# Score broadcasts on GpSimd's queue, row copies for the last batch only, and scatters issued later, in a windowed attention with a mixture-of-depths stage

## The chip, the cores and the metric

The kernel runs on one core of a Trainium2 chip. The metric is the device time of one execution in microseconds, the median over several runs. The profile is one execution recorded by the hardware profiler; its span (148.8 us for the kernel before) is a little shorter than the device time of the same run (150.53 us).

The engines are named as in the profile: PE is TensorE (matrix products; PEld its weight loads), DVE is VectorE, ACT is ScalarE, POOL is GpSimd, SP is SyncE, which here only issues transfers. Each engine takes its instructions in program order, so an instruction that waits holds up everything behind it on that engine.

## What is computed

Attention with a few sink keys and a sliding window, over 4 batches, 8 heads, 768 positions and head size 64; then a feed-forward layer on the 128 rows of each batch that score highest against a gate vector.

```python
keep = (pos[None, :] < 4) | ((rel >= 0) & (rel < 128))       # 4 sinks, a window of 128
a = softmax(where(keep, q @ k.T / 8, -1e9));  x = a @ v       # (B, S, 512) once heads are joined
scores = einsum('bsd,d->bs', x, w_gate)
out = x.copy()
for b in range(4):
    top = indices of the 128 largest scores[b]
    ye = maximum(x[b, top] @ w1, 0) @ w2                      # 512 -> 1024 -> 512
    out[b, top] = x[b, top] + sigmoid(scores[b, top])[:, None] * ye
```

## The kernel before

**Steps.** Attention is cut into 30 steps of 128 query rows: steps 0 to 11 for batch 0 (in two halves of the heads), then six steps for each of the batches 1, 2 and 3 (12 to 17, 18 to 23, 24 to 29). In step i TensorE first forms the scores of step i + 2 (`step_scores`), ScalarE takes their exponentials, then TensorE forms the sums over the values of step i (`values`, line 262, with the sink part at line 272) in PSUM banks 4 and 5. VectorE normalizes them (`norm`, lines 295 and 298) into a tile x, and the next step's `values` can't overwrite the banks before that. VectorE then forms the gate scores of the 128 rows (`gate_score`, line 302). SyncE stores x to the output (`store`, line 503).

**An order written by hand.** Everything else is hung on the steps: `before(i, ...)` runs ahead of step i, `middle(i, ...)` between its scores and its values, `at(i, ...)` after its normalization, `late(i, ...)` at its end. Loads of K and Q (line 129) and V (148, 152) go out on SyncE, K and Q are cast on GpSimd (line 141), transposed on TensorE (line 172), and the key columns of the sinks copied by GpSimd (`sink_keys`, line 186). The compiled program gives SyncE's transfers eight completion semaphores in turn: each transfer waits for the one eight places ahead of it.

**Ranking.** To find the 128 best rows of a batch, each score is compared with all 768 of the batch. For batches 0 and 1 the scores go to memory and come back on all 128 partitions: `bounce_out` (line 306) writes the column tile scol to a row srow in DRAM, `bounce_in` (line 309) reads it back into sbc, the same row on every partition. Then `rank_c` (line 312, VectorE) counts for 128 rows at a time how many scores are larger. The bounces of batch 0 are placed at steps 12 and 13, its ranks from step 15 on; those of batch 1 at steps 18 and 19, its ranks from step 20 on. For batches 2 and 3 the row is made on the chip step by step: `spread` (line 316, TensorE into bank 2, then a copy by ScalarE) and `compare` (lines 323 and 325).

**Choosing.** `select` (line 345) turns ranks into one-hot matrices, and `chosen` (line 351) multiplies them with a small table tok of token numbers and scores into a PSUM bank; VectorE copies the result to ch (line 354) and forms the row indices. `gather` (line 376) fetches the 128 chosen rows with an indirect transfer of GpSimd. For batch 0 it reads the output itself; for batches 1 to 3 it reads a second copy of the rows, xrow, which `store` writes beside the output (line 505), with indices local to the batch (idl). For these batches VectorE forms two sets of indices: idl for the gather and idx for the later scatter.

**Feed-forward.** `ffn_cast` (line 381, GpSimd), `ffn_in` (386), `ffn_1` (394), `ffn_2` (401) and `ffn_out` (406) follow two to five steps later; ffn_out adds the rows (y) and at once scatters them into the output (line 408, an indirect transfer of GpSimd). Batch 0 does this in steps 24 to 26, batch 1 in 27 to 29, batch 2 from step 29 on, batch 3 after the last step. The weights are cast while loading, on GpSimd's queue (lines 521 and 525).

Of the kernel before, what the change touches and what calls it, by code (L numbers as in the profile page):

```python
# [8 lines left out]
FP32 = mybir.dt.float32  # L9
BF16 = mybir.dt.bfloat16  # L10
I32 = mybir.dt.int32
U32 = mybir.dt.uint32
# [3 lines left out]
B = 4  # L16
H = 8
S = 768
D = 64
HP = H // 2  # L20
NB = S // 128
DM = H * D
# [11 lines left out]
def kernel(  # L34
# [14 lines left out]
    pe, dve, act, pool, sp = nc.tensor, nc.vector, nc.scalar, nc.gpsimd, nc.sync  # L49
# [35 lines left out]
    tok = [one([128, NB, 4], BF16, f"tok{i}") for i in range(B)]  # L85
    gt = [one([128, 1], FP32, f"gt{i}") for i in range(B)]
    idx = [one([128, 1], U32, f"idx{i}") for i in range(B)]
    xe = [one([128, DM], FP32, f"xe{i}") for i in range(3)]
# [17 lines left out]
    tk_i = one([128, B + 1, NB], I32, "tk_i")  # L106
    flat = out.rearrange("b s d -> (b s) d")
    srow = tc.dram_tile([B, S], FP32, name="srow")
    xrow = [None] + [tc.dram_tile([S, DM], FP32, name=f"xrow{i}") for i in range(1, B)]
    idl = [None] + [x0[:, NB - 2, 8 * i:8 * i + 1].bitcast(U32) for i in range(1, B)]  # L110

    class State:
        def __init__(self, b):
# [7 lines left out]
    st = [State(b) for b in range(B)]  # L121
# [181 lines left out]
                                 op0=ALU.mult, op1=ALU.add, accum_out=st[b].scol[:, j:j + 1])  # L303

    def bounce_out(b):
        sp.dma_start(out=srow[b, :].rearrange("(p c) -> p c", c=NB), in_=st[b].scol[:, :])

    def bounce_in(b):
        sp.dma_start(out=sbc[:, :], in_=srow[b, :].partition_broadcast(128))

    def rank_c(b, c):
        dve.tensor_scalar(out=junk[:, :].bitcast(BF16)[:, 0:S], in0=sbc[:, :], scalar1=st[b].scol[:, c:c + 1],  # L312
# [35 lines left out]
    def chosen(b, bank, e=E):  # L348
        t = tok[b]
        for c in range(NB):  # L350
            pe.matmul(out=ps[:, bank, 0:4], lhsT=e[:, c, :], rhs=t[:, c, :],
                      start=(c == 0), stop=(c == NB - 1))
        ch = jp.tile([128, 4], FP32, name="ch", tag="ch")
        dve.tensor_copy(out=ch[:, :], in_=ps[:, bank, 0:4])
        dve.tensor_scalar(out=(idl[b] if b else idx[0])[:, :], in0=ch[:, 0:1], scalar1=128.0, scalar2=ch[:, 1:2],
                          op0=ALU.mult, op1=ALU.add)
        if b:
            chl = x0[:, NB - 2, 32:33]
            dve.tensor_scalar_add(out=chl[:, :], in0=ch[:, 1:2], scalar1=float(b * S))
            dve.tensor_scalar(out=idx[b][:, :], in0=ch[:, 0:1], scalar1=128.0, scalar2=chl[:, 0:1],  # L360
                              op0=ALU.mult, op1=ALU.add)
        return ch

    def gate(b, ch):
        g = gt[b]
        dve.tensor_tensor(out=g[:, :], in0=ch[:, 2:3], in1=ch[:, 3:4], op=ALU.add)
        act.activation(out=g[:, :], in_=g[:, :], func=ACT.Exp, scale=-1.0)

    def gate_end(b):
        g = gt[b]  # L370
        dve.tensor_scalar_add(out=g[:, :], in0=g[:, :], scalar1=1.0)
        dve.reciprocal(out=g[:, :], in_=g[:, :])

    def gather(b):
        src, ix = (xrow[b], idl[b]) if b else (flat, idx[0])
        pool.indirect_dma_start(out=xe[b % 3][:, :], out_offset=None, in_=src[0:S, :],
                                in_offset=bass.IndirectOffsetOnAxis(ap=ix[:, 0:1], axis=0),
                                bounds_check=S - 1, oob_is_err=False)

    def ffn_cast(b):  # L380
        pool.tensor_copy(out=xeb[:, :], in_=xe[b % 3][:, :])

    def ffn_in(b, bank):
        trp = ps[:, bank, :].bitcast(BF16).rearrange("p (c n) -> p c n", c=8)
        for dc in range(4):
            pe.transpose(out=trp[:, dc, :], in_=xeb[:, dc * 128:(dc + 1) * 128], identity=ident_b[:, :])
        act.copy(out=xeT[:, :, :], in_=trp[:, 0:4, :])  # L387
# [10 lines left out]
    def ffn_2(b, half, bank):  # L398
        for f in range(4):
            fc = 4 * half + f  # L400
            pe.matmul(out=ps[:, bank, :], lhsT=hT[:, fc, :], rhs=w2_sb[:, fc, :],
                      start=(fc == 0), stop=(fc == 7))

    def ffn_out(b, bank):
        y = jp.tile([128, DM], FP32, name="y", tag="y")
        dve.scalar_tensor_tensor(out=y[:, :], in0=ps[:, bank, :], scalar=gt[b][:, 0:1], in1=xe[b % 3][:, :],  # L406
                                 op0=ALU.mult, op1=ALU.add)
        pool.indirect_dma_start(out=flat[0:(b + 1) * S, :],
                                out_offset=bass.IndirectOffsetOnAxis(ap=idx[b][:, 0:1], axis=0),
                                in_=y[:, :], in_offset=None, bounds_check=(b + 1) * S - 1, oob_is_err=False)  # L410

    with tc.manual_schedule():
        dve.memset(zb[:, :], 0.0)
# [11 lines left out]
                           base=0, pattern=[[-1, 128]], channel_multiplier=1)  # L425
# [47 lines left out]
        def at(i, f):  # L473
            todo.setdefault(i, []).append(f)
# [7 lines left out]
        def before(i, f):  # L482
            early.setdefault(i, []).append(f)
# [13 lines left out]
        xt = {}  # L497

        def store(i):
            b, j, g = steps[i]  # L500
            if g == 0:
                return
            sp.dma_start(out=out[b, j * 128:(j + 1) * 128, :], in_=xt[(b, j)])
            if b:
                sp.dma_start(out=xrow[b][j * 128:(j + 1) * 128, :], in_=xt[(b, j)])


        arrived = {}
# [19 lines left out]
        def choose(b, bank, e=E):  # L528
            keep[b] = chosen(b, bank, e)
            gate(b, keep[b])  # L530
            gather(b)
# [23 lines left out]
        at(26, lambda: choose(1, 3))  # L555
        late(26, lambda: select(E2, rankl[0], 0, NB))
        at(27, lambda: gate_end(1))
        at(27, lambda: choose(2, 2, E2))
        at(28, lambda: gate_end(2))
        for b in range(B - 1):  # L560
            at((12, 18, 24)[b], lambda b=b: token_cols(b))
# [22 lines left out]
        def ffn(b, i):  # L584
            before(i, lambda: ffn_cast(b))
            at(i, lambda: ffn_in(b, Y))
            at(i + 1, lambda: ffn_1(b, 0, Y + 1))
            at(i + 1, lambda: ffn_1(b, 1, Y))
            for half in range(2):
                at(i + 2, lambda half=half: ffn_2(b, half, Y + 1))  # L590
            at(i + 2, lambda: ffn_out(b, Y + 1))
        ffn(0, 24)
        ffn(1, 27)
        before(29, lambda: ffn_cast(2))
        at(29, lambda: ffn_in(2, Y))

# [4 lines left out]
                           pattern=[[-NSINK, HP]], channel_multiplier=1)  # L601
        pool.affine_select(out=o, in_=o, compare_op=ALU.is_ge, fill=0.0, base=NSINK - 1,
                           pattern=[[NSINK, HP]], channel_multiplier=-1)
# [4 lines left out]
                        in_=own4[0:16, :].unsqueeze(1).to_broadcast((16, 2 * B, HP)))  # L608
        pool.tensor_copy(out=vsk[64:80, :, :, :, :].rearrange("p b e h d -> p (b e h d)"),
                         in_=vsk[0:16, :, :, :, :].rearrange("p b e h d -> p (b e h d)"))  # L610

        for i, (b, j, g) in enumerate(steps):
            for f in early.get(i, []):
                f()
            if i:
                store(i - 1)
            step_scores(i + 2)
            for f in mid.get(i, []):
                f()
            heads = range(4) if g is None else (2 * g, 2 * g + 1)  # L620
            values(b, j, heads, X, g or 0)
            if b == 0:
                x = x0[:, j, :]
            else:
                x = xp.tile([128, DM], FP32, name="x", tag="x")[:, :]
            norm(x, heads, X)
            if i == len(steps) - 1:
                gate_score(b, j, x)
            for f in todo.get(i, []):
                f()  # L630
            if g != 0:
                xt[(b, j)] = x
                if i < len(steps) - 1:
                    gate_score(b, j, x)
                if b == B - 1:
                    pool.tensor_copy(out=xb[:, j, :], in_=x)  # L636
            for f in todo_late.get(i, []):
                f()
            if i == 5:
                pool.iota(iota_i[:, :], pattern=[[1, 128]], base=0, channel_multiplier=0)  # L640
                pool.iota(tk_i[:, 0:B, :], pattern=[[0, B], [1, NB]], base=0, channel_multiplier=0)
                pool.iota(tk_i[:, B, :], pattern=[[0, NB]], base=0, channel_multiplier=1)
            if i == 8:
                dve.tensor_copy(out=iota_f[:, :], in_=iota_i[:, :])
                for n in range(B):
                    dve.tensor_copy(out=tok[n][:, :, 0], in_=tk_i[:, n, :])
                    dve.tensor_copy(out=tok[n][:, :, 1], in_=tk_i[:, B, :])
        store(len(steps) - 1)

        b = B - 1  # L650
# [18 lines left out]
        choose(b, 2)  # L669
        ffn_2(2, 1, 0)  # L670
        ffn_out(2, 0)
        gate_end(b)
        ffn_1(b, 0, Y)
        ffn_1(b, 1, Y + 1)
        ffn_2(b, 0, 1)
        ffn_2(b, 1, 1)
        ffn_out(b, 1)


# [33 lines left out]
```

The softmax here doesn't subtract the row's maximum and nothing guards it: scores larger than these inputs give would overflow.

## Time and profile before

| | before |
|---|---|
| device time, median of 3 | 153.0 us (152.77 to 153.94) |
| span of the profiled run | 148.8 us |
| mean granted TensorE clock | 0.966 |
| busy: PE / DVE / ACT / POOL | 120.2 / 91.5 / 78.5 / 58.8 us |
| moved by DMA | 35.57 MB, mean 239 GB/s |
| SyncE's queue (q1) | 30.16 MB, 66.8% of the 16 DMA engines |
| GpSimd's queue (q0) | 4.23 MB, 13.6% |

Busy time doesn't add up to a bound: what counts is where the busiest engine waits, and for whom. The page gives, for each group of instructions, the idle time ahead of it and what ended it; a list of waits sums the same by pairs, and timelines show single instructions in order. The page's slices show that the DMA engines are busy nine tenths and more in most of the first 100 us:

```profile
PEclk9999999999999999999999997589999999999995
DMA  3999969987999999999999799899995346332031
```

Each digit is one fortieth of the span. The upper row is the clock that TensorE was granted in tenths, the lower row the busy share of the DMA engines. The clock has one dip, about 90 to 100 us from the start.

### The profile page before, as it was taken

What the parts mean: (1) busy time and instruction counts of PE and PEld (TensorE: products, weight loads), DVE (VectorE), ACT (ScalarE), POOL (GpSimd) and SP (SyncE); (2) the same over time, 40 slices, a digit from 0 to 9 for tenths busy, and PEclk for the clock granted to TensorE, in tenths of its full rate; (3) what the DMA queues carried; (4) which work ended last, traced back from release to release, by engine and by line L of the source; (5) the groups of instructions that cost most, each with busy time, mean ns of one, the idle gap of its engine ahead of it and who ended that gap; (6) DMA issues with size and microseconds to landing.
All of it is one profiled execution on the core that took longest, in us unless ns stands there. A gap on an engine that the chain in (4) does not pass through costs nothing. (4 is left out here: it accounts for less than half of the span.)

```text
span 148.8 us, 6421 instructions
## 1 busy us (share of the span) xinstructions
PE 120.2 (81%) x2755; PEld 91.6 (62%) x2759; DVE 91.5 (62%) x287; ACT 78.5 (53%) x106; POOL 58.8 (40%) x99
## 2 busy tenths in 40 slices
PE   6687989998989987669799920998989969977940
PEld 2255676787778866538588810776777558856810
DVE  6851172569438464098988306778996696688520
ACT  3169467598887875365746780055827232323310
POOL 8819404865504573343170401810111264412421
PEclk9999999999999999999999997589999999999995
DMA  3999969987999999999999799899995346332031
GB/s 100 376 222 361 213 173 365 341 207 194 286 291 375 335 240 317 352 347 348 268 327 316 221 257 317 218 194 172 279 275 195 143 148 216 141 141 77 3 138 70
DMA packets 43227, 35.57 MB, mean 239 GB/s; under 512 B 27184, under 2 KB 36400, under 8 KB 43200
## 3 DMA queue, kind: packets, MB, share of 16 engines
q1 hardware_dynamic: 40288, 30.16, 66.8%
q0 software_dynamic: 2368, 4.23, 13.6%
q10 hardware_dynamic: 544, 0.79, 1.5%
q8 instruction: 21, 0.34, 0.9%
q14 instruction: 6, 0.05, 0.1%
HBM read 25.20 MB, written 12.06 MB: 250 GB/s over the span
## 5 line engine op out<-in xcount | busy, mean ns | idle before, releaser
L251 ACT ACTIVATE pt<-ps 128x1024 f32<-128x1024 f32 x48 | 47.0, 1032 | 6.7 <-PE ps L229 6.0
L262 PE MATMUL ps<-vbuf,pt 64*64 64x65 f32 (+1 forms) x1440 | 47.6, 230 | 3.6 <-issue 2.9
L262 PEld LDWEIGHTS ps<-vbuf,pt 64*64 64x64 f32 (+1 forms) x1440 | 40.7, 139 | 15.3 <-issue 11.8
L141 POOL CAST kq<-raw 128x768 bf16<-128x768 f32 x28 | 23.4, 847 | 20.4 <-DMA raw<-in_k_dram 14.9
L295 DVE RECIPROCAL rz<-ps 128x8 f32<-128x8 f32 (+1 forms) x30 | 5.9, 196 | 29.1 <-PE ps L262 29.0
L272 PE MATMUL ps<-vsk,psk 64*64 64x260 f32 (+1 forms) x180 | 16.5, 359 | 8.6 <-DVE x L298 8.6
L213 PE MATMUL ps<-QT,KT 64*64 64x192 bf16 (+2 forms) x384 | 17.2, 243 | 5.0 <-ACT QT L179 2.6
L298 DVE TENSOR_TENSOR x<-ps,rz 128x256 f32<-128x256 f32 (+1 forms) x60 | 19.5, 366 | 1.6 <-DMA xrow<-x 0.4
L312 DVE TENSOR_SCALAR_CACHE_REDUCE junk<-sbc,scol 128x768 bf16<-128x768 f32 x12 | 12.2, 1013 | 12.3 <-DMA sbc<-srow 11.9
L302 DVE CUSTOM_DVE_ANT_0 junk<-x,wgb 128x512 f32<-128x512 f32 x24 | 18.0, 750 | 0.4
L186 POOL COPY ksk<-KT 64x4 bf16<-64x4 bf16 x32 | 8.7, 273 | 23.8 <-DVE KT L177 12.5
L179 ACT COPY QT<-ps 128x768 bf16<-128x768 bf16 x16 | 12.8, 801 | 7.9 <-PE ps L172 7.9
L213 PEld LDWEIGHTS <-KT 64*64 64x64 bf16 x384 | 10.3, 105 | 9.9 <-issue 6.0
L229 PE MATMUL ps<-mask,ident_b 64*64 64x256 bf16 (+1 forms) x208 | 15.0, 259 | 0.0
L172 PE MATMUL ps<-ident_b,kq 128*128 128x128 bf16 x192 | 13.6, 220 | 1.6 <-ACT kq L139 1.5
L272 PEld LDWEIGHTS ps<-vsk,psk 64*64 64x64 f32 x180 | 7.7, 135 | 10.3 <-DVE x L298 8.9
L172 PEld LDWEIGHTS <-kq 128*128 128x128 bf16 x192 | 11.1, 98 | 3.7 <-ACT kq L139 1.7
L318 ACT COPY sbl<-ps 128x128 f32<-128x128 f32 x12 | 3.1, 261 | 19.3 <-PE ps L316 19.3
L177 DVE COPY KT<-ps 128x768 bf16<-128x768 bf16 x10 | 9.5, 950 | 1.4 <-PE ps L172 1.4
L636 POOL CAST x<-x 128x512 bf16<-128x512 f32 x6 | 4.2, 703 | 15.1 <-DVE x L298 9.0
L394 PE MATMUL ps<-xeT,w_sb 128*128 128x128 bf16 x128 | 8.0, 219 | 0.7 <-ACT xeT L387 0.7
L394 PEld LDWEIGHTS <-w_sb 128*128 128x128 bf16 x128 | 7.4, 98 | 1.1 <-DVE y L406 0.9
(91 smaller groups left out, 133.1 us busy)
## 6 DMA issues: line engine op xcount, KB each, us to landing
out_dram<-x SPq DMA_DIRECT2D x24, 256.0 KB, 4.7
raw<-in_k_dram SPq DMA_DIRECT2D x15, 384.0 KB, 5.5
raw<-in_q_dram SPq DMA_DIRECT2D x15, 384.0 KB, 5.9
xrow<-x SPq DMA_DIRECT2D x18, 256.0 KB, 4.9
vbuf<-in_v_dram SPq DMA_DIRECT2D x33, 128.0 KB, 5.2
w_sb<-in_moe_w_dram POOLq DMA_DIRECT2D x4, 512.0 KB, 12.5
vbuf<-in_v_dram SPq DMA_DIRECT2D x2, 384.0 KB, 6.8
sbc<-srow SPq DMA_DIRECT2D x2, 384.0 KB, 6.6
```

What stands on the lines that cost most here:

```text
L141: (eng or pool).tensor_copy(out=o, in_=i)
L172: pe.transpose(out=trp[:, c, :], in_=src[:, c, :, :].rearrange("p h d -> p (h d)"), identity=ident_b[:, :])
L179: act.copy(out=o, in_=i)
L213: pe.matmul(out=sc[64 * m:64 * m + 64, e, a, o:o + n], lhsT=s.KT[r, hp, k0:k0 + 64], rhs=s.QT[r, hp, k0:k0 + n], start=a == 0, stop=False, ...
L229: pe.matmul(out=o, lhsT=ident_b[r, r], rhs=w[r].unsqueeze(1).to_broadcast((64, a.stop - a.start, 2, 64)), start=False, stop=True, skip_gro ...
L251: act.activation(out=po[:, gi, :, :, :], in_=sc[:, :, :, :], func=ACT.Exp, scale=0.125)
L262: pe.matmul(out=ps[64 * c:64 * c + 64, bank + be, hh * SK:hh * SK + SK], lhsT=p[i][rows, h, 64 * slot:64 * slot + 64], rhs=s.v[be][rows, h ...
L272: pe.matmul(out=ps[64 * c:64 * c + 64, bank + be, a * SK:z * SK], lhsT=s.psk[which][r, c, 64 * (j - 1):64 * j], rhs=vsk[r, b, be, a:z, :], ...
L298: dve.tensor_tensor(out=xo[:, e, :, :], in0=xg[:, e, :, 0:D], in1=rz[:, e, 0:n, :].to_broadcast((128, n, D)), op=ALU.mult)
L302: dve.tensor_tensor_reduce(out=junk[:, :], in0=x, in1=wgb[:, :], scale=1.0, scalar=0.0, op0=ALU.mult, op1=ALU.add, accum_out=st[b].scol[:, ...
L312: dve.tensor_scalar(out=junk[:, :].bitcast(BF16)[:, 0:S], in0=sbc[:, :], scalar1=st[b].scol[:, c:c + 1], scalar2=0.0, op0=ALU.is_gt, op1=A ...
L394: pe.matmul(out=hps[:, f, :], lhsT=w1_sb[:, dc, fc * 128:(fc + 1) * 128], rhs=xeT[:, dc, :], start=(dc == 0), stop=(dc == 3), skip_group_c ...
```

## The change

Four things are changed.

1. The two bounces of the scores of batches 0 and 1 are issued on GpSimd's queue instead of SyncE's, so that they needn't stand in SyncE's list.
2. Only the last batch keeps a second copy of its rows. Batches 1 and 2 gather from the output, with global row numbers: the table tok now holds 6b + c instead of c for batches 0 to 2, so that one set of indices serves gather and scatter.
3. A scatter to the output ahead of a gather from it would put the two in order. So the scatters of batches 0 and 1 are taken out of ffn_out and issued two steps after it for batch 0 (step 28) and at the end of the same step for batch 1 (step 29), after the gather of batch 2.
4. The third batch's `chosen` writes bank 3 instead of bank 2, which `spread` uses.

```diff
-    xrow = [None] + [tc.dram_tile([S, DM], FP32, name=f"xrow{i}") for i in range(1, B)]
-    idl = [None] + [x0[:, NB - 2, 8 * i:8 * i + 1].bitcast(U32) for i in range(1, B)]
+    xrow = tc.dram_tile([S, DM], FP32, name="xrow")
+    idl = x0[:, NB - 2, 0:1].bitcast(U32)
     def bounce_out(b):
-        sp.dma_start(out=srow[b, :].rearrange("(p c) -> p c", c=NB), in_=st[b].scol[:, :])
+        pool.dma_start(out=srow[b, :].rearrange("(p c) -> p c", c=NB), in_=st[b].scol[:, :])
     def bounce_in(b):
-        sp.dma_start(out=sbc[:, :], in_=srow[b, :].partition_broadcast(128))
+        pool.dma_start(out=sbc[:, :], in_=srow[b, :].partition_broadcast(128))
...
+        last = b == B - 1
-        dve.tensor_scalar(out=(idl[b] if b else idx[0])[:, :], ...)
-        if b:
+        dve.tensor_scalar(out=(idl if last else idx[b])[:, :], ...)
+        if last:
...
     def gather(b):
-        src, ix = (xrow[b], idl[b]) if b else (flat, idx[0])
+        src, ix, n = (xrow, idl, S) if b == B - 1 else (flat, idx[b], (b + 1) * S)
...
     def ffn_out(b, bank):
         ...
+    def scatter(b):
         pool.indirect_dma_start(out=flat[0:(b + 1) * S, :], ...)
...
     def store(i):
-            if b:
-                sp.dma_start(out=xrow[b][j * 128:(j + 1) * 128, :], in_=xt[(b, j)])
+            if b == B - 1:
+                sp.dma_start(out=xrow[j * 128:(j + 1) * 128, :], in_=xt[(b, j)])
...
-        at(27, lambda: choose(2, 2, E2))
+        at(27, lambda: choose(2, 3, E2))
...
+        late(28, lambda: scatter(0))
+        late(29, lambda: scatter(1))
...
-                pool.iota(tk_i[:, 0:B, :], pattern=[[0, B], [1, NB]], base=0, channel_multiplier=0)
+                pool.iota(tk_i[:, 0:B, :], pattern=[[NB, B], [1, NB]], base=0, channel_multiplier=0)
```

After the last step the scatters of batches 2 and 3 directly follow their ffn_out, as before.

More of the change, by code (lines that the diff above doesn't have):

```diff
@@ L354, in chosen @@
         dve.tensor_copy(out=ch[:, :], in_=ps[:, bank, 0:4])
-        dve.tensor_scalar(out=(idl[b] if b else idx[0])[:, :], in0=ch[:, 0:1], scalar1=128.0, scalar2=ch[:, 1:2],
+        last = b == B - 1
+        dve.tensor_scalar(out=(idl if last else idx[b])[:, :], in0=ch[:, 0:1], scalar1=128.0, scalar2=ch[:, 1:2],
                           op0=ALU.mult, op1=ALU.add)
-        if b:
+        if last:
             chl = x0[:, NB - 2, 32:33]
@@ L374, in gather @@
     def gather(b):
-        src, ix = (xrow[b], idl[b]) if b else (flat, idx[0])
-        pool.indirect_dma_start(out=xe[b % 3][:, :], out_offset=None, in_=src[0:S, :],
+        src, ix, n = (xrow, idl, S) if b == B - 1 else (flat, idx[b], (b + 1) * S)
+        pool.indirect_dma_start(out=xe[b % 3][:, :], out_offset=None, in_=src[0:n, :],
                                 in_offset=bass.IndirectOffsetOnAxis(ap=ix[:, 0:1], axis=0),
-                                bounds_check=S - 1, oob_is_err=False)
+                                bounds_check=n - 1, oob_is_err=False)
     def ffn_cast(b):
@@ L402, in ffn_2 @@
                       start=(fc == 0), stop=(fc == 7))
+    ys = {}
     def ffn_out(b, bank):
-        y = jp.tile([128, DM], FP32, name="y", tag="y")
+        y = ys[b] = jp.tile([128, DM], FP32, name="y", tag="y")
         dve.scalar_tensor_tensor(out=y[:, :], in0=ps[:, bank, :], scalar=gt[b][:, 0:1], in1=xe[b % 3][:, :],
                                  op0=ALU.mult, op1=ALU.add)
+    def scatter(b):
         pool.indirect_dma_start(out=flat[0:(b + 1) * S, :],
                                 out_offset=bass.IndirectOffsetOnAxis(ap=idx[b][:, 0:1], axis=0),
-                                in_=y[:, :], in_offset=None, bounds_check=(b + 1) * S - 1, oob_is_err=False)
+                                in_=ys[b][:, :], in_offset=None, bounds_check=(b + 1) * S - 1, oob_is_err=False)
     with tc.manual_schedule():
@@ L645 @@
                 for n in range(B):
-                    dve.tensor_copy(out=tok[n][:, :, 0], in_=tk_i[:, n, :])
+                    dve.tensor_copy(out=tok[n][:, :, 0], in_=tk_i[:, n % (B - 1), :])
                     dve.tensor_copy(out=tok[n][:, :, 1], in_=tk_i[:, B, :])
@@ L671 @@
         ffn_out(2, 0)
+        scatter(2)
         gate_end(b)
@@ L677 @@
         ffn_out(b, 1)
+        scatter(b)
 _INS = ['q', 'k', 'v', 'n_sink', 'window', 'moe_w_gate', 'moe_w1', 'moe_w2', 'moe_capacity']
```

## The prediction

> **What bounds the kernel now.** I read the busy shares first. TensorE is busy 81% of the span, so it sets the pace, and time is won where it stands still. The list of waits then shows who makes it stand still.
>
> ```profile
> PE 120.2 (81%) x2755; PEld 91.6 (62%) x2759; DVE 91.5 (62%) x287; ACT 78.5 (53%) x106; POOL 58.8 (40%) x99
> DVE junk L312 <- DMA sbc<-srow: 11.9, 2, 7.6
> PE ps L272 <- DVE x L298: 8.6, 5, 5.5
> ```
>
> Two waits of VectorE for the score broadcast make 11.9 us, the longer one 7.6. TensorE's waits for x (line 298, the normalization, also on VectorE) make 8.6, the longest 5.5. The timelines tie them together; columns are start, length, engine, line, operation, and in brackets the idle time before it with its releaser.
>
> ```profile
> 63.00 1.01 DVE L312 TENSOR_SCALAR_CACHE_REDUCE junk<-sbc,scol 128x768 bf16<-128x768 f32 x1 [4.27 <-DMA sbc<-srow]
> 65.70 0.99 PE L272 MATMUL ps<-vsk,psk 64*64 64x260 f32 x8 [1.34 <-DVE x L298]
> ...
> 82.98 0.08 DVE L302 DVE_READ_ACCUMULATOR2_ANT scol<- 128x1 f32 x1
> 90.70 1.01 DVE L312 TENSOR_SCALAR_CACHE_REDUCE junk<-sbc,scol 128x768 bf16<-128x768 f32 x1 [7.63 <-DMA sbc<-srow]
> ...
> 92.93 1.46 PE L272 MATMUL ps<-vsk,psk 64*64 64x260 f32 x8 [5.47 <-DVE x L298]
> ```
>
> VectorE is in order. The normalization of step 21, whose sums TensorE had ready at about 84.7, stands behind line 312 until 92.2, and TensorE can't reuse the PSUM banks. In the table of stretches (time, busy of PE, PEld, DVE, ACT, POOL, granted clock, DMA share, GB/s) the stall also costs clock:
>
> ```profile
> 80.20:92.20 12.00, 6.34 (x166) 5.24 (x165) 4.26 (x14) 6.51 (x10) 2.36 (x5) 0.94 0.92 270
> 92.20:97.50 5.30, 4.57 (x73) 3.53 (x74) 3.54 (x14) 0.00 (x0) 3.62 (x5) 0.50 0.87 231
> ```
>
> Why is the broadcast late? The scores of batch 1 are complete at 70.5 (end of the row product of step 17, 70.46 + 0.08). SyncE's queue shows the rest:
>
> ```profile
> 80.22 0.41 SPq L306 DMA_DIRECT2D srow<-scol  x1
> 83.97 0.32 SPq L309 DMA_DIRECT2D sbc<-srow  x1
> ```
>
> The store of the scores is issued 9.7 us after they exist. SyncE is behind with its list: DMA share is 1.04, 1.08, 1.06 in 43-57, 57-66, 66-80.2, and in the compiled order each of its transfers waits for the one eight places before (eight completion semaphores in turn). Issue to landing of a broadcast is 6.6 us.
>
> [...] a gather on GpSimd's queue issued at 82.4, beside a full SyncE queue and the broadcast, took 7.7 us, three later ones 3.4 to 3.6. [...] the trace shows such issues at 1.05 to 1.63 us. [...]
>
> **The change, part by part.**
>
> *Bounces on GpSimd, batch 1.* GpSimd reaches the store after its casts at 69.16 to 71.2, against 80.2 on SyncE. Landing took 4.8 to 6.6 for a srow store; I take 5, so 76.2. GpSimd meanwhile does the key copies at 74.81 and two casts up to 77.3, then issues the broadcast; all of this moves about 1.5 us earlier with the items below, so call it 75.8. Its landing is bounded by 3.6 (an unloaded gather of 256 KB) and 7.7 (the loaded one); 5.6 is my value[...]. It lands at 79.4 to 83.5, middle 81.4. VectorE asks at 83.06 less the shift of 1, 82. Even at 83.5 the normalization of step 21 ends (1.7 us of rank and compare, 1.0 of normalization) at 86.2, and TensorE, still busy with transposes and scores to 87.45 less 1, isn't held. So the 5.47 us go, and with them the half clock: the eight line-272 matmuls took 1.46 instead of 0.61 (+0.85), the 64 of line 262 ran from 94.32 to 97.40, 3.08 instead of 1.78 (+1.30). Sum 7.6.
>
> *Bounces, batch 0.* Here GpSimd is no earlier at the store (after a cast ending at 50.9, against 51.38): its casts wait for loads. With 4.8 to land, GpSimd waits to about 55.7, issues, and 5.6 later it is 61.3 against 63.0. Without a stall line 312 would have to start by 60.9, since two of them take 2.1 and TensorE's sums of step 16 end at 63.03. I take 0.9 of the 1.34. Queued behind GpSimd's wait are four key copies (54.0) and the casts at 59.05. The copies serve the sink scores at 62.95, the casts transposes at 70.90; both have room.
>
> *Twelve row copies of 256 KB less (batches 1 and 2), and four bounces less on SyncE.* 3.1 MB at about 310 GB/s are 10 us of DMA time, nearly all in 55 to 106. This itself moves nothing on the path: loads are early enough (the cast of the last pair ends at 77.3, its transposes are at 84.95). What it does is to let SyncE keep up once the steps come faster. Without it the loads would follow a list that is 9.7 us late.
>
> *Gathers from the output.* The same 128 rows of 2 KB, same stores waited for. For batches 1 and 2 two small VectorE operations fall away, about 0.3 us ahead of each gather.
>
> *Scatters later.* Moved behind casts; 1.0 to 1.2 us of GpSimd each. Scatter 0 waits for gather 2, but so does the cast next to it. That cast ended at 128.2, its transposes ran at 131.91, which hides one issue. Scatter 1 still follows line 406 of step 29. The last two scatters stay: the final one waits in the same way for scatter 2 and for y (143.35 + 0.75). Nothing.
>
> *Third batch chosen in bank 3.* Removes TensorE's 1.22 us before 122.40, where spread waited for the copy of bank 2. After it comes ffn_in, which needs the cast ending at 121.76 (about 0.3 earlier now), so 0.9 is left.
>
> Sum: 7.6 + 0.9 + 0.9 = 9.4 us; 153.0 - 9.4 = **143.6 us**.
>
> **New waits looked at.** The weights: GpSimd issued them at 93.57 to 96.6 with 7.3 to 18.1 us to land, the last about 114, and line 401 needs it from 116.14 on. In the new kernel they go out after the key copies of step 21, at about 86 (7.6 earlier), while the demand comes about 8.5 earlier, with less traffic beside them. Tight, up to 1 us. Gather 0 holds GpSimd's key copies (5.92 us before 90.20): issued near 81, landing at 85 to 88.5; the sink scores that need the copies come at about 88.5 to 89. No cost, or under 1 us.
>
> **The rivals.**
>
> *The broadcast is as slow on GpSimd's queue, or slower (20%).* For: 7.7 us of the gather; casts waiting for loads may hold the store[...]. Against: the start alone is 8 us earlier. Landing at 87 instead of 83.4 gives back 3.6 us, and 0.9 of batch 0: 148.1 with the clock kept.
>
> *More than counted (15%).* VectorE falls behind no more in steps 17 and 18 (TensorE waits of 0.27 and 0.86), and waits labelled "issue" inside line 262 (0.74 at 55.59, 1.21 at 62.34) shrink with less traffic. 1.13 + 1.0 + 0.4 for all of batch 0: 141.1.
>
> *Not faster (7%).* Each broadcast makes GpSimd wait for its store, 4.8 to 6.6 us. Were all that stands behind it on the path, two such waits would add 13.2 us against the 9.4 won, less the 2.83 that GpSimd idles before 58.28 anyway: 153.0 + 13.2 - 9.4 - 2.8 = 154. Against it: the slack of over 7 us between casts and transposes.
>
> **How the numbers follow.** 58% for the main case at 143.6, 20, 15 and 7 for the others. The low end takes the third case and half a microsecond more, 140.5. The high end is the second case, 148.0. Faster by over 1% 0.91, within 1% 0.04, slower 0.05.
>
> **What will show it.** Line 312's wait for sbc under 3 us in sum instead of 11.9; no TensorE wait for x over 2 us; granted clock at 0.9 or more in mid-span; the store of the scores of batch 1 issued on GpSimd near 70; no TensorE wait in front of line 316 behind the copy ch. I am wrong if the broadcast still lands after VectorE asks by over 2 us, if GpSimd's wait for srow is followed by a TensorE wait for KT or QT, or if line 394 or 401 waits for weights.

## The result, and the profile after

The changed kernel takes **145.6 us** in the median of 4 runs (145.04 to 151.22); the kernel before, beside it, 152.88 (152.13 to 153.94). The ratio is 0.946, 95% interval 0.936 to 0.956. Run again on other occasions it took 142.78 (ratio 0.963, 0.943 to 0.982) and 145.59 (0.961, 0.940 to 0.981), beside 151.08 and 152.98 before. The forecast was 143.6 in a range of 140.5 to 148.0. Runs of one kernel spread by several us, so medians here are over all its runs and ratios over the faster ones alone (within 1.5% of its fastest), and the trace read below is that of the second occasion (142.85 us, span 141.1), not that of the first (151.22).

The page's busy shares, clock row and DMA row, then two lines of the list of waits (who waited for what: us in sum, times, longest):

```profile
PE 118.6 (84%) x2755; PEld 90.5 (64%) x2759; DVE 89.5 (63%) x283; ACT 78.7 (56%) x106; POOL 61.4 (43%) x103
PEclk9999999999999999999999999999999999999998
DMA  3999969997989999999898997499993526351131
DVE junk L312 <- DMA sbc<-srow: 0.4, 1, 0.4
PE ps L272 <- DVE x L298: 1.4, 3, 0.5
```

TensorE still does the same work (118.6 us for 120.2), but the clock row has no dip left (the row of the third occasion stands at 6 and 8 from 64.5 to 71.7 us, another place, and at 5 from 7.2 to 10.8). VectorE's wait for the broadcast has gone from 11.9 us to 0.4, TensorE's wait for x from 8.6 to 1.4, the longest from 5.5 to 0.5. The timelines of GpSimd and VectorE around the second broadcast:

```profile
72.03 0.55 POOL L306 DMA_DIRECT2D srow<-scol  x1 [2.37 <-DVE scol L302]
78.43 0.54 POOL L309 DMA_DIRECT2D sbc<-srow  x1
...
84.56 1.01 DVE L312 TENSOR_SCALAR_CACHE_REDUCE junk<-sbc,scol 128x768 bf16<-128x768 f32 x1
86.81 0.21 DVE L295 RECIPROCAL rz<-ps 128x8 f32<-128x8 f32 x1 [0.64 <-PE ps L262]
```

The scores are stored at 72.03 instead of 80.22 and broadcast at 78.43 instead of 83.97. The second broadcast takes 4.7 us from issue to landing, so it is there at 83.1; line 312 starts at 84.56 without a wait that the profile shows, and the normalization of step 21 waits for TensorE's sums, not TensorE for it.

To compare kernels whose steps shift, I cut each span at VectorE's normalizations (line 295) of steps 12, 15, 18 and so on. The stages in us, with the kernels of the experiments:

| kernel | 12-15 | 15-18 | 18-21 | 21-24 | 24-27 | 27-29 | rest | span |
|---|---|---|---|---|---|---|---|---|
| before | 12.4 | 15.6 | 19.7 | 13.0 | 15.8 | 9.0 | 18.8 | 148.8 |
| changed, first occasion | 15.9 | 12.4 | 12.5 | 12.6 | 17.8 | 8.3 | 20.0 | 149.5 |
| changed, second occasion | 14.8 | 14.1 | 13.0 | 12.5 | 14.9 | 8.2 | 18.8 | 141.1 |
| changed, third occasion | 12.4 | 15.7 | 13.0 | 12.5 | 14.9 | 8.3 | 20.0 | 143.4 |
| bounces alone | 12.1 | 15.2 | 12.9 | 13.1 | 19.8 | 9.0 | 19.0 | 148.1 |
| bounces, weights earlier | 13.0 | 14.9 | 14.4 | 12.5 | 19.4 | 9.0 | 20.1 | 149.0 |
| bank 3 alone | 13.2 | 13.9 | 19.9 | 12.9 | 15.6 | 8.1 | 18.8 | 147.8 |
| ranks later | 13.2 | 13.9 | 12.9 | 14.9 | 19.3 | 9.0 | 20.0 | 148.6 |
| all but the bounces | 11.8 | 14.8 | 14.4 | 11.1 | 15.2 | 8.0 | 18.7 | 141.2 |
| all but the bounces, again | 11.3 | 14.8 | 17.9 | 12.8 | 15.3 | 8.3 | 19.9 | 145.4 |
| tiny copies | 12.4 | 13.6 | 19.8 | 12.8 | 15.0 | 8.4 | 20.0 | 148.6 |
| copies on GpSimd | 14.3 | 14.0 | 14.1 | 11.1 | 21.2 | 8.3 | 20.5 | 153.4 |
| changed, bank 2 | 12.1 | 14.9 | 13.0 | 12.5 | 15.2 | 9.0 | 20.1 | 144.6 |
| scatters at once | 14.6 | 15.2 | 13.3 | 12.6 | 15.6 | 13.3 | 19.6 | 149.3 |

Most of the gain is in 18-21 (6.7 us); 21-24, 24-27 and 27-29 give 0.5, 0.9 and 0.7 to 0.8 on the second and third occasions. What is before step 12 is left out: the first normalization came at 13.8 to 16.8 us in these traces, 13.76, 15.46 and 16.80 in those of the unaltered changed kernel. That scatter at the start belongs to no edit, and single stages scatter too: 12-15 is 12.4, 14.8 and 15.9 in three traces of the changed kernel, and 24-27 is 17.8 in the first of them, where no engine waits for weights and a TensorE wait of 1.54 us has no releaser in the profile. So a stage is read below together with the wait that explains it.

So far all is as forecast. The row for the bounces alone shows that the division among the edits is not.

### The profile page after: what moved, and what is told of

Its sections match the earlier page's. It is cut to its first block, busy times and chain, and to the rows that moved or that the text cites. A ratio compares the mean times of both kernels' runs of the same rounds, so it can differ in the third digit from the quotient of the medians.

```text
span 149.5 us, 6406 instructions
## 1 busy us (share of the span) xinstructions
PE 122.4 (82%) x2759; PEld 93.0 (62%) x2759; DVE 90.3 (60%) x283; ACT 79.0 (53%) x106; POOL 60.8 (41%) x103
## 3 DMA queue, kind: packets, MB, share of 16 engines
q0 software_dynamic: 2592, 5.02, 14.9%
## 5 line engine op out<-in xcount | busy, mean ns | idle before, releaser
L262 PEld LDWEIGHTS ps<-vbuf,pt 64*64 64x64 f32 (+1 forms) x1440 | 40.1, 135 | 19.5 <-issue 15.5
L186 POOL COPY ksk<-KT 64x4 bf16<-64x4 bf16 x32 | 9.3, 292 | 38.2 <-DVE KT L177 27.5
L141 POOL CAST kq<-raw 128x768 bf16<-128x768 f32 x28 | 22.6, 849 | 2.0 <-DMA raw<-in_k_dram 1.5
L213 PE MATMUL ps<-QT,KT 64*64 64x192 bf16 (+2 forms) x384 | 17.8, 249 | 5.1 <-ACT QT L179 2.4
L179 ACT COPY QT<-ps 128x768 bf16<-128x768 bf16 x16 | 12.8, 803 | 11.6 <-PE ps L172 11.6
L272 PE MATMUL ps<-vsk,psk 64*64 64x260 f32 (+1 forms) x180 | 15.6, 346 | 1.7 <-DVE x L298 1.4
L213 PEld LDWEIGHTS <-KT 64*64 64x64 bf16 x384 | 10.6, 108 | 10.3 <-issue 6.1
L172 PE MATMUL ps<-ident_b,kq 128*128 128x128 bf16 x192 | 14.6, 228 | 2.9 <-ACT kq L139 2.0
L172 PEld LDWEIGHTS <-kq 128*128 128x128 bf16 x192 | 11.9, 102 | 4.9 <-ACT kq L139 2.2
L643 POOL CAST x<-x 128x512 bf16<-128x512 f32 x6 | 4.7, 790 | 15.8 <-DVE x L298 9.8
L395 PE MATMUL ps<-xeT,w_sb 128*128 128x128 bf16 x128 | 9.4, 239 | 0.7 <-ACT xeT L388 0.7
L318 ACT COPY sbl<-ps 128x128 f32<-128x128 f32 x12 | 3.1, 262 | 12.1 <-PE ps L316 12.1
L395 PEld LDWEIGHTS <-w_sb 128*128 128x128 bf16 x128 | 8.8, 109 | 1.1 <-DVE y L409 0.8
```

The lines of the kernel that those rows point to most:

```text
L141: (eng or pool).tensor_copy(out=o, in_=i)
L172: pe.transpose(out=trp[:, c, :], in_=src[:, c, :, :].rearrange("p h d -> p (h d)"), identity=ident_b[:, :])
L179: act.copy(out=o, in_=i)
L213: pe.matmul(out=sc[64 * m:64 * m + 64, e, a, o:o + n], lhsT=s.KT[r, hp, k0:k0 + 64], rhs=s.QT[r, hp, k0:k0 + n], start=a == 0, stop=False, ...
L262: pe.matmul(out=ps[64 * c:64 * c + 64, bank + be, hh * SK:hh * SK + SK], lhsT=p[i][rows, h, 64 * slot:64 * slot + 64], rhs=s.v[be][rows, h ...
L272: pe.matmul(out=ps[64 * c:64 * c + 64, bank + be, a * SK:z * SK], lhsT=s.psk[which][r, c, 64 * (j - 1):64 * j], rhs=vsk[r, b, be, a:z, :], ...
```

## The experiments

My theory was the prediction's: the broadcast's new queue ends a stall of 7.6 us, and the removed copies move nothing. The rival: the copies that are gone bring the gain, through the DMA traffic.

**The changed kernel again**, so that all stands beside the same runs of before. 142.78 us, as shown above, a little under the range; from step 12 to step 29 it takes 77.5 us instead of 85.4.

> The changed kernel once more, for a trace without the late start of the first one (there batch 0 ended 5.4 us later than in the trace of before, in code that the change doesn't touch). Theory (the change pays by ending VectorE's two waits for the score broadcast): 143.5 to 146 us, both waits at 0, no TensorE wait for x over 2 us, clock above 0.9 in every stretch, and 7 to 9 us less than before between the normalizations of step 12 and step 29. Rival (the gain was elsewhere, in fewer bytes): the waits for the broadcast stay at 2 us or more, and the gain is spread over many small waits.

**The bounces alone**: the kernel before, with one edit.

```diff
-        sp.dma_start(out=srow[b, :].rearrange("(p c) -> p c", c=NB), in_=st[b].scol[:, :])
+        pool.dma_start(out=srow[b, :].rearrange("(p c) -> p c", c=NB), in_=st[b].scol[:, :])
-        sp.dma_start(out=sbc[:, :], in_=srow[b, :].partition_broadcast(128))
+        pool.dma_start(out=sbc[:, :], in_=srow[b, :].partition_broadcast(128))
```

> The kernel before with only the two bounces moved to GpSimd's queue; all row copies stay. Theory: the place in SyncE's list is what made the broadcast late, so this alone brings most of the gain, 6.5 to 8.5 us of it: 145 to 147 us. Rival (SyncE's list and the bytes of the row copies are what counts): a broadcast on GpSimd's queue beside a full SyncE list takes as long as the gather did (7.7 us) and little is won, 149 us or more, or SyncE's lateness now holds loads and the stall moves to another wait.

149.2 us (147.53 to 152.36), beside 151.08; ratio 1.002 (0.973 to 1.031). The edit that was to bring 7.6 or 8.5 us brings 1.9 by the medians and nothing by the ratio. Yet its own mechanism works: stage 18-21 falls to 12.9. The loss is in 24-27, 19.8 for 15.8. Timelines of GpSimd (the issues of the MoE weights) and TensorE in this kernel, and the weights' landing in the view of the tile w_sb:

```profile
94.96 1.52 POOL L521 DMA_DIRECT2D w_sb<-in_moe_w_dram  x2 [4.19 <-DMA vbuf<-in_v_dram]
96.46 1.53 POOL L525 DMA_DIRECT2D w_sb<-in_moe_w_dram  x2
...
106.69 3.31 PE L394 MATMUL ps<-xeT,w_sb 128*128 128x128 bf16 x30 [1.33 <-DMA w_sb<-in_moe_w_dram]
116.10 1.02 PE L401 MATMUL ps<-w_sb,hT 128*128 128x512 bf16 x4 [1.73 <-DMA w_sb<-in_moe_w_dram]
...
DMA to landing us min/median/max: 7.6/13.2/18.8
```

TensorE comes to the FFN of batch 0 earlier and stands before weights that have not landed: 1.33 us at line 394, at half clock after it (mean granted clock 0.53 from 106.6 to 110.1; 3.31 us for 30 matmuls, where 32 took 1.95 before), and 1.73 at line 401. The same lines of the kernel before:

```profile
93.57 1.49 POOL L521 DMA_DIRECT2D w_sb<-in_moe_w_dram  x2 [2.72 <-DMA vbuf<-in_v_dram]
95.04 1.54 POOL L525 DMA_DIRECT2D w_sb<-in_moe_w_dram  x2
...
110.43 1.95 PE L394 MATMUL ps<-xeT,w_sb 128*128 128x128 bf16 x32
116.14 1.89 PE L401 MATMUL ps<-w_sb,hT 128*128 128x512 bf16 x7
...
DMA to landing us min/median/max: 7.3/12.5/18.1
```

The landing time grows from issue to issue (7.3, 10.6, 14.3 and 18.1 us), so there the last weights landed at 95.8 + 18.1 = 113.9, 2.2 us before line 401 starts and about 3 before its second half, which needs them. That was all the room there was. With the bounces alone they land at 97.2 + 18.8 = 116.0, and the second half of line 401 starts at 116.10. Having won 6.8 us in stage 18-21, the bounces alone run into the weights.

**All but the bounces**: the changed kernel with both bounces back on SyncE.

```diff
-        pool.dma_start(out=srow[b, :].rearrange("(p c) -> p c", c=NB), in_=st[b].scol[:, :])
+        sp.dma_start(out=srow[b, :].rearrange("(p c) -> p c", c=NB), in_=st[b].scol[:, :])
-        pool.dma_start(out=sbc[:, :], in_=srow[b, :].partition_broadcast(128))
+        sp.dma_start(out=sbc[:, :], in_=srow[b, :].partition_broadcast(128))
```

> The changed kernel with the two bounces back on SyncE's queue: twelve row copies less, scatters later, bank 3. Theory: SyncE's list is shorter by 3 to 4 copies ahead of the second bounce of batch 1 (about 4 us), so the 7.6 us wait of VectorE shrinks to about 3 to 4, which hides almost wholly behind TensorE's own work of that step: 146 to 149 us, the first wait (4.3 us) unchanged. Rival (bytes decide): as fast as the changed kernel within 1%. Rival (only the queue decides): 151 us or more.

143.62 us (142.93 to 144.3); ratio 0.972 (0.958 to 0.985), only 0.8 us behind the changed kernel on the same occasion (1.4 us by the ratios). The rival's number. SyncE's queue, TensorE's wait for x and VectorE's for the broadcast in this kernel, then the weights' landing:

```profile
78.98 0.38 SPq L306 DMA_DIRECT2D srow<-scol  x1
81.49 0.34 SPq L309 DMA_DIRECT2D sbc<-srow  x1
...
89.03 0.98 PE L272 MATMUL ps<-vsk,psk 64*64 64x260 f32 x8 [0.49 <-DVE x L298]
DVE junk L312 <- DMA sbc<-srow: 3.6, 2, 2.6
...
DMA to landing us min/median/max: 6.5/11.4/16.0
```

SyncE stores the scores 7.1 us after they exist instead of 9.7. With 3.1 MB less to move, the broadcast is issued 2.5 us after the store instead of 3.75 and takes 5.2 us instead of 6.6: it is there at 86.7 instead of 90.6, and TensorE waits 0.49 us instead of 5.47. The weights, issued up to 93.8, have landed at 109.8, when line 402, which starts at 109.6, is still at its first half, for which they aren't needed. Nobody waits for them. So without the copies both places are cured, though the bounces stay on SyncE. The other edits of this kernel can't have done it: the gathers, scatters and the bank differ only from the second gather on, which is issued at 110.90.

**Bank 3 alone**: the kernel before, with this line.

```diff
-        at(27, lambda: choose(2, 2, E2))
+        at(27, lambda: choose(2, 3, E2))
```

> The kernel before with only the third batch chosen in bank 3. Theory: TensorE's wait of 1.22 us before the spread of step 27 goes, 0.9 of it is kept: 151.5 to 152.5 us. Rival (the feed-forward input is tied to the cast and the gather and takes it all back): 152.5 to 153, no difference that can be measured.

149.65 us; ratio 1.011 (0.996 to 1.026): unclear from times, and under both ranges, which were set from 153.0 us for the kernel before, while it took 151.08 on this occasion. In its trace 27-29 is 8.1 for 9.0, as priced; the first normalization alone scatters by more than that. But the table bears it out: 27-29 is 9.0 in all five traces with bank 2 and 8.0 to 8.4 in all with bank 3, except where the scatters go at once. A second test of the bank follows below.

**Bounces with the weights earlier**, on top of the bounces' edit. If only the weights' issue is late, issuing them after an earlier value load should free the bounces' gain.

```diff
-                    after(i, arrived[(B - 1, 5)])
+                    after(i, arrived[(B - 1, 3)])
```

> The bounces on GpSimd's queue with all row copies kept, and the load of the weights tied to the V load of two steps earlier (chunk 3 of batch 3 instead of chunk 5). The trace of the bounces alone had no wait for the broadcast left on TensorE, but TensorE waited for weights (1.33 and 1.73 us) and ran the first weight products at half clock (3.31 instead of 1.95 us), since GpSimd held the weights 4.19 us for a V load late in SyncE's list. Theory (SyncE's lateness turned into a wait for the weights): this gives 3 to 4.5 us back against the bounces alone, 144.5 to 146.5 us. Rival (the bytes of the copies slow everything a little): 148 us or more, with no single wait to show for it.

150.3 us (20 runs), beside 152.59 (39 runs); ratio 0.986 (0.979 to 0.992). A gain of about 1.5% (1.0 us between the lowest times, 147.22 and 148.24), and not the 3 to 4.5 us against the bounces alone. Timelines of GpSimd and TensorE, and the view of w_sb:

```profile
91.84 1.51 POOL L521 DMA_DIRECT2D w_sb<-in_moe_w_dram  x2
93.33 1.53 POOL L525 DMA_DIRECT2D w_sb<-in_moe_w_dram  x2
...
114.28 1.31 PE L401 MATMUL ps<-w_sb,hT 128*128 128x512 bf16 x4 [2.72 <-DMA w_sb<-in_moe_w_dram]
...
DMA to landing us min/median/max: 9.6/14.9/20.2
```

Issued 3.1 us earlier than with the bounces alone, the last weights land 1.7 us earlier, at 94.1 + 20.2 = 114.3 for 116.0. Of both figures 1.3 us is only the earlier start of this trace (step 12 is normalized at 45.6 for 47.0). Most of the earlier issue goes into a longer landing. What is moved beside them counts for more: in the five traces with the copies in SyncE's list the last weights take 17.0 to 20.2 us to land, in the seven without these copies 14.0 to 16.0. The page of before has the DMA row at 9 in most slices up to 110 us, and a DMA share of 0.87 from 92.2 to 97.5 and of 1.11 from 97.5 to 109.8, while its last weights took 18.1 us to land. This run agrees: the weights' landing on GpSimd's queue is long, 20.2 us, while SyncE's queue carries the copies.

**VectorE asks later, bounces as before.** Here the stall is taken away without touching a transfer: line 312's work is put one or two steps later in the kernel before.

```diff
-        for b, i, js in ((0, 12, (15, 15, 16, 17, 17, 18)), (1, 18, (20, 21, 22, 23, 24, 25))):
+        for b, i, js in ((0, 12, (16, 16, 17, 17, 18, 18)), (1, 18, (22, 22, 23, 23, 24, 25))):
```

> The kernel before with the ranks of batches 0 and 1 hung one and two steps later (steps 16 to 18 and 22 to 25), the broadcasts left where they are. Theory (VectorE's order turns a late broadcast into a TensorE stall): the wait of 7.6 us falls under 2 us and TensorE's 5.5 us stall goes, as with the bounces alone; and as there the weights then take most of it back: 147.5 to 149.5 us, with TensorE waiting for w_sb. If the broadcast itself is what costs (its traffic), the time stays as before, 150.5 to 152 us.

151.63 us (20 runs) beside 152.59, but ratio 1.011 (1.004 to 1.018): no gain by either measure over 1 us. The time lies in the range of the other theory, that the broadcast's traffic is what costs; the trace speaks for the first. The wait for the broadcast is gone, and 18-21 is 12.9. TensorE's timeline shows where it went:

```profile
107.97 3.32 PE L394 MATMUL ps<-xeT,w_sb 128*128 128x128 bf16 x30 [1.91 <-DMA w_sb<-in_moe_w_dram]
```

With 24-27 at 19.3, this second way of ending the stall meets the same weights, and they take back all of the gain, where I expected most of it. That makes the limit a property of the kernel with the copies, not of GpSimd's queue.

**Copies that carry little.** The copies save SyncE twelve issues as well as the bytes. All but the bounces, with the twelve copies back in SyncE's list, 16 columns each, into a tile that nobody reads:

```diff
+            elif b:
+                r = (b - 1) * S + j * 128
+                sp.dma_start(out=xcopy[r:r + 128, 0:16], in_=xt[(b, j)][:, 0:16])
```

> The changed kernel with the bounces on SyncE, and on SyncE's list twelve copies of 64 bytes a row (of 2,048) for batches 1 and 2 that nobody reads: the list is as long as before, without the bytes. If the number of transfers in the list counts (eight in flight, each waiting for the one eight places before), it is as slow as before, 149 to 152 us. If the bytes count, it stays within 1.5 us of the kernel without them, 143 to 145.5 us. I expect the bytes, with up to 1 us for the twelve issues.

146.85 us (144.67 to 150.33), ratio 0.971 (0.935 to 1.008): between the two expectations, and the interval holds both. The one trace is of the run of 150.33 us; in it the weights have landed at 95.4 + 15.2 = 110.6 and nobody waits for them, but SyncE issues the store of the scores at 80.89, 10.3 us after they exist (9.7 before), and stage 18-21 is 19.8. So without their bytes the copies no longer delay the weights in this trace. Whether their mere places in SyncE's list delay the broadcast stays open: this trace has the delay, but the fastest run, 144.67, can hardly have had all of it.

**The bytes on GpSimd's queue.** The same copies, whole, away from SyncE:

```diff
+            elif b:
+                r = (b - 1) * S + j * 128
+                pool.dma_start(out=xcopy[r:r + 128, :], in_=xt[(b, j)])
```

> The same, but with twelve whole copies (256 KB each, nobody reads them) on GpSimd's queue: the bytes are back, SyncE's list stays short. Theory that the bytes count whatever the queue: 148 us or more, SyncE's loads late again, VectorE's wait for the second broadcast 5 us or more. Theory that only SyncE's own order counts: 143 to 146 us.

154.75 us (150.04 to 155.47), beside 152.59: the gain is gone. But not by the way I wanted to test. The weights are in time (97.3 + 15.5 = 112.8, and no engine waits for them; three of the twelve copies are issued only after them). VectorE waits 1.9 us for the second broadcast, not 5 or more, and SyncE stores the scores 4.7 us after they exist: with the copies out of its list SyncE is less late, whatever the bytes elsewhere. Beside the tiny copies (10.3 us late, places without bytes) this points to the places in the list as what holds the broadcast, one trace each. TensorE loses 3.78 us in 24-27 (21.2 us) and clock too (the 64 matmuls of line 263 take 3.08 us from 115.89, and 1.78 from 104.99), after VectorE stood 5.52 us inside the normalization of step 25:

```profile
113.48 0.76 DVE L299 TENSOR_TENSOR x<-ps,rz 128x256 f32<-128x256 f32 x2 [5.52 <-issue]
114.35 0.53 PE L214 MATMUL ps<-QT,KT 64*64 64x192 bf16 x7 [3.78 <-DVE rankl L337]
```

The profile names no releaser. Probably the buffer of x was still held by a copy queued behind the weights on GpSimd (copies were issued right after them, from 98.0); that is argued, not shown. The run says that the bytes can't simply go to another queue, and little on the weights.

**The near pairs once more, on the third occasion.** First the changed kernel and all but the bounces.

> The changed kernel, beside the next three on one chip. Both theories: 5 to 8 us under the kernel before.

> The changed kernel with the bounces on SyncE once more, to size what their move adds once the copies are gone. First theory of the prediction (the bounces carry the gain): 4 us or more slower than the changed kernel. Theory from the runs so far (the bytes of the copies carry it, and end both SyncE's lateness and the late weights): 0 to 2 us slower, with VectorE's wait for the second broadcast 2 to 4 us and weights landing before TensorE asks.

145.59 (144.07 to 148.87) and 146.18 (144.45 to 147.12), beside 152.98; ratios 0.961 (0.940 to 0.981) and 0.964 (0.948 to 0.979). Both theories' range for the changed kernel holds (7.4 us under before). Again the bounces add 0.6 us, which these runs can't tell from none. They do something that the traces show. All but the bounces on this occasion, TensorE's timeline and VectorE's wait:

```profile
89.80 1.46 PE L272 MATMUL ps<-vsk,psk 64*64 64x260 f32 x8 [3.94 <-DVE x L298]
DVE junk L312 <- DMA sbc<-srow: 9.5, 2, 6.1
```

On SyncE the broadcast can still be late by 6.1 us even without the copies, where I expected 2 to 4. With both edits TensorE never waited over 0.55 us for x, in three traces of the changed kernel and in the two of its variants below. So the move to GpSimd probably takes this chance away; what it is worth on average these runs don't size.

**The bank, undone in the changed kernel.**

```diff
-        at(27, lambda: choose(2, 3, E2))
+        at(27, lambda: choose(2, 2, E2))
```

> The changed kernel with the third batch chosen in bank 2 as before. Theory: TensorE's wait of 1.2 us before the spread of step 27 is back and steps 27 to 29 take 9.0 us instead of 8.0 to 8.3: 0.7 to 1 us slower. Rival: hidden, less than 0.3 us.

146.38 us against 145.59, ratio 0.968 (0.955 to 0.982): 0.8 us, with intervals that overlap. The trace has the wait back, and 27-29 at 9.0 for 8.3:

```profile
116.95 0.49 PE L316 MATMUL ps<-ident_f,scol 128*128 128x128 f32 x2 [1.24 <-DVE ch L354]
```

**Scatters at once**, where ffn_out used to issue them.

```diff
+            at(i + 2, lambda: scatter(b))
-        late(28, lambda: scatter(0))
-        late(29, lambda: scatter(1))
```

> The changed kernel with scatters 0 and 1 at once after their sums, as before; now gather 2 has to wait for scatter 0, since both touch the output. By the trace of the changed kernel the sums of batch 0 are there about 6 us before gather 2 is issued and a scatter lands in 3.2 us, so I expect no loss, within 0.7 us. Rival (the order gather behind scatter costs): gather 2 lands later and with it the cast and the input of batch 2, 1 to 3 us slower.

150.93 us (147.6 to 151.97), against 145.59; ratio 0.983 (0.950 to 1.017), against 0.961. I expected no difference; it is 5.3 us slower by the medians and 3.5 by the ratios, whose intervals overlap. The trace has the loss in 27-29 (13.3 for 8.3). GpSimd's and TensorE's timelines:

```profile
112.70 1.09 POOL L377 DMA_INDIRECT xe<-out_dram,idx  x1 [4.81 <-DVE gt L367]
117.09 1.07 POOL L413 DMA_INDIRECT out_dram<-y,idx  x1 [3.30 <-DVE x L298]
118.71 1.09 POOL L382 CAST xeb<-xe 128x512 bf16<-128x512 f32 x1
121.53 1.05 POOL L377 DMA_INDIRECT xe<-out_dram,idx  x1 [1.73 <-issue]
...
119.86 0.61 PE L387 MATMUL ps<-ident_b,xeb 128*128 128x128 bf16 x4 [3.05 <-POOL xeb L382]
```

The y of batch 0 was ready at 114.1, yet the scatter went out at 117.09. GpSimd stood 3.30 us before it. The scatter writes the output that gather 1, issued at 112.70, still reads until about 116.2 (my estimate, from the 3.4 to 3.6 us that gathers took in the changed kernel's first trace), and stands for that landing (for the rest of the wait the profile names the normalization of line 298); the cast of batch 1 stands behind it in GpSimd's order and starts at 118.71. In the changed kernel that cast started at 114.26 (second occasion) and 115.04 (third). TensorE waits 3.05 us for it instead of 0.27, and its clock falls: the 64 matmuls of line 262 take 3.08 us from 121.47, where the step before took 1.78, and the mean granted clock from 106 to 124 is 0.85. Gather 2 in turn goes out at 121.53 instead of at 116.05, after the scatter of 117.09 has landed (at 119.8 to 120.9 by the 2.7 to 3.8 us of the scatters in that first trace, my estimate).

## Why the prediction was right, and where it was not

- *Bounces, batch 1: 7.6 us.* The mechanism and the size hold: 18-21 and 21-24 together fell by 7.2 us (32.7 to 25.5), the half clock (0.50 from 92.2 to 97.5) went with the stall, the store came at 72.03 ("near 70"), and the landing, forecast for 79.4 to 83.5, was 83.1. The 5.6 us in that forecast were an estimate, between the 3.6 and 7.7 us of two gathers; it took 4.7. One reading was off: of the "4.8 to 6.6" for landing a store of the scores, 6.6 is the broadcast's, and the store took 4.8 before, and after 4.8 in the median on the second occasion, 5.4 and 3.7 on the first. But the gain was credited to one edit. Alone, the bounces won the same 6.8 us in 18-21 and gave 4.0 back in 24-27.
- *The step that failed: twelve row copies less.* "This itself moves nothing on the path: loads are early enough." I looked at the loads of K, Q and V and not at the weights, which landed beside the copies (DMA share 0.87 to 1.11 from 92.2 to 109.8) and had 2 to 3 us of room. Without the copies the weights' last landing went from 113.9 to 106.4, ahead of line 402; with bounces or later ranks alone it stayed at 114.3 to 116.0. The lines of the changed kernel:

```profile
89.19 1.52 POOL L526 DMA_DIRECT2D w_sb<-in_moe_w_dram  x2
90.69 1.52 POOL L530 DMA_DIRECT2D w_sb<-in_moe_w_dram  x2
...
104.12 1.95 PE L395 MATMUL ps<-xeT,w_sb 128*128 128x128 bf16 x32
109.29 1.89 PE L402 MATMUL ps<-w_sb,hT 128*128 128x512 bf16 x7
...
DMA to landing us min/median/max: 5.4/10.1/15.0
```

  The last issue is at 91.4 and lands at 91.4 + 15.0 = 106.4, 2.9 us before line 402 starts. Part of this is the issue, 4.4 us earlier, and part the shorter landing, 15.0 us for 18.1. And without copies the old broadcast too came 3.9 us sooner. Taken alone, all but the bounces brings 6.8 to 7.5 us by the medians and 4.3 to 5.6 by the ratios, of which by the bank's pair 0.8 is the bank's.
- *"The weights … tight, up to 1 us."* No wait for them in the changed kernel; the reason given, less traffic beside them, fits the shorter landing. The prediction priced this traffic at nothing in an earlier step, so the two steps contradict each other. Had I asked what the second gives without the copies, I'd have found the 24-27 loss.
- *Bounces, batch 0: 0.9 us.* Not seen. Stage 15-18 is 12.4, 14.1 and 15.7 in the changed kernel, 15.6 before, and 13.9 to 14.8 in kernels that leave these bounces on SyncE (bank alone, all but the bounces). VectorE's wait for that broadcast was 0, 0.4 and 2.0 us in these three traces. TensorE's 1.34 us wait for x is gone, but in two of them a wait of 1.75 us inside line 262 stands in the same stage.
- *Bank 3: 0.9 us.* 0.7 to 0.9 in the stage, 0.8 between medians.
- *Gather 0, "no cost, or under 1 us".* Issued at 83.79, landed 4.8 us later; no wait of TensorE stands behind it.
- *Scatters later: "Nothing".* Right as a cost, but its role was not in the sum: it is what makes *gathers from the output* free. Left where they were, scatters cost 3.5 us by the ratios and 5.3 by the medians.
- *Rivals.* "As slow on GpSimd's queue" fell: 4.7 to 6.3 us in one trace, 7.0 for the first broadcast of the other, and the second starts 5.5 us earlier. "More than counted" is not shown; the best occasion, 142.78, is within the scatter of the main case. "Not faster" fell: what is queued behind GpSimd's wait for srow had the room that was claimed.

The total was right since the whole change was made, and that is luck in its division: the weights came in time through an edit that the sum has at nothing. By its own working the prediction would have given the bounces alone 8.5 us, and missed by over 6.

## What to carry to other kernels

When a stall is taken away, list who next needs a transfer, with the landing and the need of each: here the second limit stood 2 to 3 us behind the first, and ended two quite different cures. Where the DMA row is full for tens of us, as here, bytes taken off it are not "off the path": they can set when other transfers land (here the last weights: 15.0 us after their issue, and 18.1 with the copies), and issuing an urgent one earlier can buy little (here 3.1 us earlier gave 1.7, with 1.3 of both from the start of the trace). An edit that frees a buffer of its readers (gathering from the output) may need a second edit that keeps its writers back (3.5 us by the ratios here, 5.3 by the medians); price the two together.

## What the runs showed of the hardware

- The broadcast of 3 KB to 128 partitions shows no fixed price for its queue. The second one took 4.2 to 5.0 us from issue to landing on GpSimd's queue (with the copies still there 4.2 and 5.0), on SyncE's 6.3 to 6.6 with the copies and 5.2 without (all but the bounces). The first took 6.3 to 7.8 us on GpSimd's queue and 4.9 in the only trace that has it on SyncE's. They were issued at different times beside different traffic; which counts more, queue or traffic, isn't shown.
- Order on an engine: in the kernel before, TensorE's sums of step 21 were there at 84.7 us, and VectorE began their normalization at 92.22, behind line 312's wait of 7.63 us. Eight places in SyncE's list: of 103 transfers in that trace, all for which it records the landing of the one eight places ahead, none was issued before that landing; with seven places, 32 of 104 were.
- Half clock came after waits of TensorE of different lengths. In the kernel before it began at 90.8 us, inside the wait of 5.47 us, and lasted to 97.6. In the changed kernel's first trace a wait of 1.54 us ended at 108.18, and the clock was at half from 109.8 to 113.2. With ranks later 1.91 us were followed by 30 matmuls in 3.32 us (111 ns each, against 61 in the kernel before), at a mean granted clock of 0.53. In the bounces with earlier weights the wait was 2.72 us, and the clock fell only when TensorE was at work again. The table of stretches of that kernel (time, busy of PE, PEld, DVE, ACT, POOL, granted clock, DMA share, GB/s):

```profile
111.60:114.20 2.60, 0.00 (x0) 0.00 (x0) 0.17 (x2) 0.36 (x2) 1.08 (x1) 1.00 0.96 293
114.20:114.80 0.60, 0.52 (x3) 0.28 (x3) 0.00 (x0) 0.00 (x0) 0.00 (x0) 1.00 0.78 307
114.80:115.40 0.60, 0.60 (x3) 0.01 (x1) 0.00 (x0) 0.00 (x0) 0.00 (x0) 0.56 0.13 51
115.40:116.00 0.60, 0.60 (x19) 0.48 (x20) 0.37 (x1) 0.00 (x0) 0.00 (x0) 0.50 0.03 14
116.00:117.00 1.00, 1.00 (x30) 0.98 (x24) 1.00 (x4) 0.58 (x1) 0.33 (x1) 0.50 0.00 0
117.00:118.00 1.00, 1.00 (x12) 0.25 (x6) 1.00 (x2) 1.00 (x2) 1.00 (x2) 0.50 0.00 0
```

  The clock column is 1.00 through the idle stretch, 0.56 in 114.8 to 115.4 and 0.50 after that, when TensorE is fully busy. A wait doesn't always bring it: the 1.73 us before line 401 in the bounces alone were followed by four matmuls in 1.02 us and, from 118.26, the 64 of line 262 in 1.78, as at full clock in the kernel before. What tells the two apart these runs don't show. So a wait of 1.3 to 2.7 us costs its own length and, when half clock follows, up to 1.7 us more, paid by work that comes after it (my estimate: half of the 3.41 us that half clock lasted in the changed kernel's first trace).
